# Earlier inputs, later weights and TensorE additions in the prologue of a Fourier-filter and mixer kernel

## The chip, the cores and the metric

One core of a Trainium2 chip. The metric is device time in microseconds (us), the median of several executions of the whole program. A ratio is the mean time of one kernel's runs over that of the other's of the same rounds on the same chip, so it is not quite the ratio of the medians quoted beside it.

Names: PE is TensorE, DVE is VectorE, ACT is ScalarE, POOL is GpSimd, SP is SyncE. PEld is a weight load of TensorE. "L216" is line 216 of the kernel in question; line numbers differ between kernels.

## The reference

```python
# x (8, 3008, 256); the four mixer weights arrive as float64
X = np.fft.rfft(x, axis=1)
y = np.fft.irfft(X * (filt_r + 1j * filt_i)[None], n=3008, axis=1)     # filter
h = np.maximum(y.transpose(0, 2, 1) @ w_tok1, 0.0) @ w_tok2             # w_tok1 (3008, 256)
u = y + h.transpose(0, 2, 1)
out = u + np.maximum(u @ w_ch1, 0.0) @ w_ch2
```

The kernel computes the transforms as matmuls in two factors (47 x 64): first transform, z through memory, filter, g through memory, then the mixer. The weights come as 64-bit numbers. The kernel reads them as pairs of 32-bit words and rounds each to float32 as the sum of two parts, "top" and "rest".

## The kernel before: the parts that matter

Instructions are issued to each engine in the order in which the program emits them. The prologue makes the first input's filter (`dft(GROUPS[0])`) and, between its steps, rounds the token weights tile by tile; each `next(convert)` rounds one tile and issues the load of a later one.

```python
    def rounded(st, n, parts, late=False):
        # ... both = a pair of buffers (hp holds two pairs), top and rest in it
        nc.scalar.activation(out=top, in_=hi_f, func=AF.Copy, scale=2.0 ** -112)      # ScalarE starts it
        nc.vector.tensor_scalar(out=top_i, ...)                                       # four VectorE steps
        nc.vector.scalar_tensor_tensor(out=top_i, ...)                                # top is ready here
        nc.vector.tensor_scalar(out=rest_i, ...)
        nc.vector.scalar_tensor_tensor(out=rest, ...)
        for src, dst in parts:
            nc.vector.tensor_tensor(out=dst, in0=src(top), in1=src(rest), op=ALU.add) # the addition

    def w1_fold(i):                      # w_tok1 alone: times the inverse transform's first factor
        nc.tensor.matmul(ps, wai_t, w, start=True, stop=True)
        nc.scalar.copy(out=w, in_=ps)

        # filter, one step k: b_unit(k) and bi_unit(k - 1)
        nc.tensor.matmul(ps, wbs[...], t2s[...])                  # ps_b, ps_pg
        nc.vector.tensor_tensor(out=p1, in0=ps, in1=fr, op=ALU.mult)
        nc.vector.scalar_tensor_tensor(out=p2[re], ...)           # - im * fi
        nc.vector.tensor_tensor(out=p2[im], ...)                  # re * fi
        nc.vector.tensor_tensor(out=p1, in0=p1, in1=p2, op=ALU.add)
        # ...
        nc.tensor.matmul(ps[0:KR], wis[...], prods.pop(k), start=True, stop=True)     # ps_acc
        nc.scalar.copy(out=t3s[c][:, r]..., in_=ps[0:KR]...)

        # prologue
        load(AHEAD)                                               # six weight tiles at once, then x
        # ... every step that converts:
                next(convert)                                     # round a tile, load another
                folds.append(len(folds))
                if len(folds) > 2:
                    w1_fold(len(folds) - 3)                       # then fold the tile of two steps ago
        # ... after the filter: w_tok2's 16 tiles
        for i in range(TC * N2 // NG):
            next(convert)
            if i == 2:
                acc = token_sums(0)                               # 48 products, 96 matmul instructions
        h1s[0] = token_relu(acc)
```

Of the kernel before, what the change touches and what calls it, by code (L numbers as in the profile page):

```python
# [45 lines left out]
AHEAD = 6  # L46
# [3 lines left out]
def _make_tables():  # L50








    n2 = np.arange(N2)
    wa = np.zeros((P, P))  # L60
    wai = np.zeros((P, P))
    for h in range(2):
        r = slice(h * 64, h * 64 + 64)
        for k2 in range(K2):
            th = 2 * np.pi * ((n2 * k2) % N2) / N2
            c, s = np.cos(th), np.sin(th)
            re, im = 4 * k2 + 2 * h, 4 * k2 + 2 * h + 1
            wa[r, re] = c
            wai[re, r] = c * (1.0 if k2 == 0 else 2.0)
            if k2 == 0:  # L70
                alt = 1.0 - 2.0 * (n2 % 2)
                wa[r, im] = alt
                wai[im, r] = alt
            else:
                wa[r, im] = -s
                wai[im, r] = -2.0 * s
    n1 = np.arange(N1)
    re = (n1 // A) * (2 * A) + n1 % A
    im = re + A
    wb = np.zeros((KR, K2, P))  # L80
    wi = np.zeros((P, K2, KR))
    for k2 in range(K2):
        for s in range(2 * A):
            if s < A:
                k, sign, q = k2 + 64 * s, 1.0, s
            else:
                j = s - A + 1
                k, sign, q = 64 * j - (k2 if k2 else 32), -1.0, 32 + s - A
                if j == A and k2:
                    continue  # L90
            th = 2 * np.pi * ((n1 * k) % N) / N
            c, sn = np.cos(th), np.sin(th)
            edge = k in (0, NF - 1)
            if edge:
                sn = np.zeros(N1)
            if k2:
                wb[re, k2, q] = c
                wb[im, k2, q] = sign * sn
                wb[re, k2, HALF + q] = -sn
                wb[im, k2, HALF + q] = sign * c  # L100
            else:
                src = re if s < A else im
                wb[src, k2, q] = c
                wb[src, k2, HALF + q] = -sn
                m = 1.0 if edge else 2.0
                wi[q, k2, src] = m * c
                wi[HALF + q, k2, src] = -m * sn
    wi[:, 1:, :] = wb[:, 1:, :].transpose(2, 1, 0)
    wi /= N
    f = np.float32  # L110
    return wa.astype(f), wai.astype(f), wb.astype(f), wi.astype(f)
# [3 lines left out]
def kernel(  # L115
# [13 lines left out]
    wa_np, wai_np, wb_np, wi_np = _make_tables()  # L129
# [4 lines left out]
    wi_d = nc.inline_tensor(wi_np, name="wi_t").ap()  # L134

# [32 lines left out]
    wai_t = glob.tile([P, P], FP32, name="wai_t")  # L168

# [35 lines left out]
    def rounded(st, n, parts, late=False):  # L205
# [3 lines left out]
        if late:  # L209

            top = p1p.tile([P, 512], FP32, tag="p1", name="top")[:, 0:n]
            rest = p2p.tile([P, 512], FP32, tag="p2", name="rest")[:, 0:n]
        else:
            both = hp.tile([P, 2, 512], FP32, tag="hh", name="both")
            top, rest = both[:, 0, 0:n], both[:, 1, 0:n]
# [9 lines left out]
        nc.vector.scalar_tensor_tensor(out=rest, in0=lo, scalar=2.0 ** -52, in1=rest, op0=ALU.mult, op1=ALU.mult)  # L225
        for src, dst in parts:
            nc.vector.tensor_tensor(out=dst, in0=src(top), in1=src(rest), op=ALU.add)

    def w1_load(i):
        st = stage(512)  # L230
        rows = moe_w_tok1.rearrange("(n2 n1) t -> n2 n1 t", n1=N1)
        last = 2 * i + 2 == A
        if last:
            nc.gpsimd.memset(st.bitcast(U32)[HALF:P, 512:1024], 0)
        for h in range(2):
            n = 1 if last and h else 2
            lo = h * A + 2 * i
            nc.gpsimd.dma_start(st[h * HALF:(h + 1) * HALF, 0:n * DT].rearrange("p (a t) -> p a t", t=DT),
                                rows[:, lo:lo + n, :])
        yield  # L240
        rounded(st, 512, [(lambda v: v, w1[:, 2 * i:2 * i + 2, :].rearrange("p a t -> p (a t)"))])

    def w1_fold(i):

        ps = bank("po%d" % (i % 2))
        w = w1[:, 2 * i:2 * i + 2, :].rearrange("p a t -> p (a t)")
        nc.tensor.matmul(ps, wai_t, w, start=True, stop=True)
        nc.scalar.copy(out=w, in_=ps)

    def w2_load(i):  # L250
# [16 lines left out]
        rounded(st, n, [(both, dst[:, :, :, ds(g * NG, NG)]), (some(w, 1), w2[:, t, ds(w * P + g * NG, NG)].unsqueeze(1))])  # L267
# [39 lines left out]
    def weights():  # L307

        steps = ([w1_load(i) for i in range(A // 2)] + [w2_load(i) for i in range(TC * N2 // NG)]
                 + [wc1_load(c * (DC // 512), False) for c in range(DH)])  # L310
        n = len(steps)
        steps += [f(i) for f, i in LAST]
        loads = iter(steps)

        def load(k):
            for _, s in zip(range(k), loads):
                next(s)

        load(AHEAD)
        yield  # L320
        for i, s in enumerate(steps):
            next(s, None)

            load(not n - 2 <= i < n)
            yield
# [5 lines left out]
    def x_load(b, c):  # L331
        last = c == NXC - 1
        t = xp.tile([P, XC, D], FP32, tag="x", name="x")
# [20 lines left out]
    def dft(bs):  # L354
# [3 lines left out]
        for u in todo[0:XB]:  # L358
            x_load(*u)
        for i, u in enumerate(todo):  # L360
            a_unit(*u, ("acc", "b")[i % 2] if first else "b")
            if i + XB < len(todo):
                x_load(*todo[i + XB])
# [16 lines left out]
        def b_unit(k):  # L380
# [7 lines left out]
            p1 = p1p.tile([P, nb, D], FP32, tag="p1", name="p1")  # L388
            p2 = p2p.tile([P, nb, D], FP32, tag="p2", name="p2")
# [3 lines left out]
            nc.vector.tensor_tensor(out=p1, in0=p1, in1=p2, op=ALU.add)  # L393
            prods[k] = p1

        def bi_unit(k):
            ps = bank("acc").rearrange("p (b d) -> p b d", b=2)[:, 0:nb, :]
            nc.tensor.matmul(ps[0:KR], wis[k // WC][:, k % WC, :], prods.pop(k), start=True, stop=True)  # L398
# [199 lines left out]
    def mix(b, next_ready, convert):  # L598
# [13 lines left out]
        for i in range(n + 1):  # L612
            now, old = i < n, i >= 1
            next(convert, None)
# [14 lines left out]
            next(convert, None)  # L629
# [29 lines left out]
    with tc.manual_schedule():  # L659
# [3 lines left out]
        convert = weights()  # L663
        next(convert)
        folds = []
        for i, _ in enumerate(dft(GROUPS[0])):
            if i == 0:
                for t, src in ((wai_t, wait_d), (wai, wai_d)):
                    nc.scalar.dma_start(t, src)

            if i % 2 == 1 and i < NXC or i % 3 == 2 and NXC < i <= NXC + 3 * (A // 4):
                next(convert)
                folds.append(len(folds))
                if len(folds) > 2:
                    w1_fold(len(folds) - 3)
        for c in range(A // TC4):
            t4_load(0, c)
        for i in range(TC * N2 // NG):
            next(convert)
            if i < 2:  # L680
                w1_fold(A // 2 - 2 + i)
            if i == 2:
                acc = token_sums(0)
        h1s[0] = token_relu(acc)
        for _ in range(DH):
            next(convert)
# [4 lines left out]
        for bs, after in zip(GROUPS, GROUPS[1:] + ((),)):  # L691
            todo = dft(after) if after else iter(())
            done = not after
            for b in bs:
# [3 lines left out]
                for i, _ in enumerate(mix(b, next_ready, convert)):  # L698
# [34 lines left out]
```

## Time and profile before

| | before |
|---|---|
| median, 4 runs | 2668.18 us (2663.97 to 2670.58) |
| stage A: to the first filter matmul | 62.0 us |
| stage B: to VectorE's last filter product | 83.2 us |
| tail: to VectorE's first sum for the mixer | 57.8 us (mixer starts at 203.1) |
| the mixer, to the end | 2464.8 us |

These borders are read from the timeline of the profiled run (span 2667.9 us). In all tables below they are taken in the same way: the first matmul on ps_b from t and wb, the start of the last filter product that writes p (the addition after it, where there is one, is not counted), the start of the first sum v from u. The prediction calls the tail stage C and counts to the mixer's first matmul (202.2 us), one us earlier. A timeline row reads: start, length, engine, line, operation, output<-input, shapes, count, and in brackets the idle time of that engine before the row with what ended it.

### The profile page before, as it was taken

Reading aid. Unit: us, or ns where it says so; the run is one execution under the profiler, and the core shown is the slowest. Engines: PE = TensorE matmul, PEld = TensorE weight load, DVE = VectorE, ACT = ScalarE, POOL = GpSimd, SP = SyncE. Lnnn points to the kernel's source line nnn. Section 1 sums busy time; section 2 is a strip of 40 time slices with the busy share of each in tenths; the row PEclk is TensorE's granted clock in tenths of the full one; section 3 lists DMA queues with packets and bytes.
Section 4 is the critical chain, followed back from the end, with each engine's and each line's share of the span. In section 5 each row is a group of like instructions: output and inputs, shape, how many; then the busy total and the mean of one; then the engine's idle time right before and its main releaser. Section 6 shows DMA issues by size and latency. Waiting matters only on the chain.

```text
span 2667.9 us, 31511 instructions
## 1 busy us (share of the span) xinstructions
PE 2511.5 (94%) x10840; PEld 1997.6 (75%) x10840; DVE 1825.9 (68%) x3505; ACT 677.4 (25%) x1325; POOL 503.4 (19%) x926
## 2 busy tenths in 40 slices
PE   4666999999999999999999999999999999999997
PEld 1344766687787777788877777788888888888886
DVE  3886588846567688745658588755678586647675
ACT  2222322212322222212322122222222122212221
POOL 2324211111212111121121112121121111211221
PEclk8778999999999999999999999999999999999999
DMA  8663344322332222212233223211322211100000
GB/s 219 190 188 111 114 119 122 96 77 79 96 103 83 72 78 75 70 32 63 90 99 89 66 84 85 79 33 41 103 70 79 55 46 56 24 9 8 17 15 17
DMA packets 167158, 210.28 MB, mean 79 GB/s; under 512 B 35868, under 2 KB 115633, under 8 KB 166998
## 3 DMA queue, kind: packets, MB, share of 16 engines
q1 hardware_dynamic: 92937, 111.56, 14.4%
q0 software_dynamic: 30976, 44.53, 6.9%
q10 hardware_dynamic: 43085, 52.17, 6.0%
q8 instruction: 86, 1.41, 0.2%
q14 instruction: 74, 0.61, 0.1%
HBM read 133.15 MB, written 74.97 MB: 78 GB/s over the span
## 4 chain that ended last, share of the span: by engine, by line
PE 71%; DVE 16%; issue 2%; ACT 2%; DMA 0%; SPq 0%; DVEq 0%; POOL 0%; ACTq 0%; POOLq 0%
PE ps_po L526 24%; PE ps_pg L492 14%; PE ps_pg L508 11%; PE ps_acc L452 6%; PE ps_acc L435 5%; DVE t L470 3%; PE ps_acc L457 3%; DVE hh L470 3%; PE ps_b L382 2%; PE ps_b L349 2%; PE ps_acc L398 2%; DVE u L470 2%; DVE s L470 2%; DVE p L392 1%; DVE p L391 1%
## 5 line engine op out<-in xcount | busy, mean ns | idle before, releaser
L470 DVE TENSOR_TENSOR hh<-ps_pg,s 128x512 f32<-128x512 f32 (+3 forms) x864 | 482.6, 586 | 639.7 <-ACT s L495 639.7
L571 POOL DMA_DIRECT2D out_dram<-r x757 | 409.7, 550 | 1971.5 <-ACT hh L513 855.6
L513 ACT ACTIVATE hh<-hh 128x512 f32<-128x512 f32 (+1 forms) x576 | 347.9, 621 | 1141.6 <-DVE hh L470 1141.6
L526 PE MATMUL ps_po<-t,wc 128*128 128x256 f32 (+1 forms) x2304 | 535.8, 375 | 3.7 <-DVE t L470 2.4
L526 PEld LDWEIGHTS ps_po<-t,wc 128*128 128x128 f32 x2304 | 434.4, 190 | 128.3 <-issue 50.4
L492 PE MATMUL ps_pg<-v,wc 128*128 128x256 f32 (+1 forms) x1728 | 417.5, 378 | 1.5 <-DVE v L470 1.5
L526 PE MATMUL ps_po<-hh,wc 128*128 128x256 f32 (+1 forms) x1728 | 413.3, 375 | 3.1 <-ACT hh L513 3.1
L492 PEld LDWEIGHTS ps_pg<-v,wc 128*128 128x128 f32 x1728 | 330.5, 192 | 42.5 <-DVE v L470 1.9
L526 PEld LDWEIGHTS ps_po<-hh,wc 128*128 128x128 f32 x1728 | 328.2, 190 | 42.2 <-ACT hh L513 5.1
L508 PE MATMUL ps_pg<-u,wc 128*128 128x256 f32 (+1 forms) x1152 | 294.3, 378 | 16.0 <-DVE hh L470 15.7
L470 DVE TENSOR_TENSOR t<-t,hh 128x256 f32<-128x256 f32 (+1 forms) x576 | 243.5, 423 | 19.8
L508 PEld LDWEIGHTS ps_pg<-u,wc 128*128 128x128 f32 x1152 | 215.3, 190 | 52.8 <-DVE hh L470 28.6
L470 DVE TENSOR_TENSOR s<-ps_pg,hh 128x512 f32<-128x512 f32 (+1 forms) x288 | 196.1, 681 | 30.0
L452 PE MATMUL ps_acc<-w,h 128*128 128x512 f32 (+1 forms) x384 | 181.7, 596 | 15.8 <-ACT h L441 11.6
L470 DVE TENSOR_TENSOR t<-hh 128x512 f32<-128x512 f32 (+1 forms) x288 | 193.1, 671 | 0.6 <-ACT hh L513 0.6
L435 PE MATMUL ps_acc<-t,w 128*128 128x256 f32 x768 | 169.5, 383 | 6.3 <-DMA t<-g_tmp 5.0
L492 PE MATMUL ps_pg<-u,wc 128*128 128x256 f32 (+1 forms) x576 | 172.4, 381 | 0.4 <-DVE hh L470 0.4
L398 PE MATMUL ps_acc<-p,wi 128*96 128x512 f32 (+1 forms) x320 | 148.2, 546 | 23.7 <-DVE p L393 12.3
L508 PE MATMUL ps_pg<-v,wc 128*128 128x256 f32 (+1 forms) x576 | 169.2, 375 | 0.0
L435 PEld LDWEIGHTS ps_acc<-t,w 128*128 128x128 f32 x768 | 147.1, 192 | 28.1 <-issue 5.8
L382 PE MATMUL ps_b<-t,wb 96*128 96x512 f32 (+1 forms) x288 | 132.7, 542 | 23.2 <-DVE p L392 11.4
L495 ACT COPY s<-ps_pg 128x256 f32<-128x256 f32 (+1 forms) x288 | 105.8, 367 | 148.6 <-PE ps_pg L492 144.5
(67 smaller groups left out, 1947.5 us busy)
## 6 DMA issues: line engine op xcount, KB each, us to landing
z_tmp<-t ACTq DMA_DIRECT2D x96, 256.0 KB
t<-z_tmp SPq DMA_DIRECT2D x128, 192.0 KB
g_tmp<-t ACTq DMA_DIRECT2D x128, 192.0 KB
t<-g_tmp SPq DMA_DIRECT2D x48, 512.0 KB
x<-in_x_dram SPq DMA_DIRECT2D x184, 128.0 KB
out_dram<-r POOLq DMA_DIRECT2D x698, 32.0 KB, 1.8
wb<-wb_t SPq DMA_DIRECT2D x80, 96.0 KB
wi<-wi_t SPq DMA_DIRECT2D x80, 96.0 KB
```

The lines of the kernel that those rows point to most:

```text
L382: nc.tensor.matmul(ps, wbs[k // WC][:, k % WC, :], t2s[k // KC][:, k % KC], start=True, stop=True)
L398: nc.tensor.matmul(ps[0:KR], wis[k // WC][:, k % WC, :], prods.pop(k), start=True, stop=True)
L435: nc.tensor.matmul(acc[:, t, :], w1[:, a, ts(t, P)], t4[b, a // TC4][:, a % TC4, :], start=(a == 0 and t == 0), stop=(a == A - 1 and t == ...
L452: nc.tensor.matmul(ps[:, 0:w], h1[:, t, ts(dh, P)], w2[:, t, ds(m * 512, w)], start=(t == 0), stop=False)
L457: nc.tensor.matmul(ps[:, ds(q * P, n)], t4[b, c][:, r, ts(dh, P)], wai[:, 0:n], start=False, stop=(q == 3))
L470: nc.vector.tensor_tensor(out=out, in0=in0, in1=in1, op=op)
L492: nc.tensor.matmul(ps[:, 0:hw], wc1[:, jp, n, :], mov, start=True, stop=True)
L495: nc.scalar.copy(out=s[:, 0], in_=g[0][:, 0, 0:hw])
L508: nc.tensor.matmul(ps[:, 0:hw], wc1[:, jp, n, :], mov, start=True, stop=True)
L513: nc.scalar.activation(out=hs, in_=hs, func=AF.Relu)
L526: nc.tensor.matmul(po[i][:, j, 0:hw], wc2[:, jp, n, :], mov, start=(jp == 0 and first == 1), stop=(jp == JP - 1 and last == 1))
L571: q.dma_start(rows[g, e, :, ds(h * A + 4 * m, n)], blocks[ts(g, CW), h, e, 0:n])
```

## The change

Its intent: let x arrive before the weights do, so that the filter starts earlier; and take work from VectorE, which is the fullest engine of the prologue, by letting TensorE add. A matmul accumulates in PSUM, so the product with top and the product with rest give the product with their sum. w_tok1 needed a product anyway; w_tok2 gets one with the identity. Likewise the filter's two products p1 and p2 are each multiplied by the second transform's factor and added in PSUM.

```diff
+    spare = [(hp, "hh"), (hp, "hh"), (rp, "r")]          # three buffer pairs
+    behind, banks = [], ["po%d" % i for i in range(4)]
+    def on_chip(stat, top, rest, n, parts):
+        # ... appended to behind, run later:
+            nc.tensor.matmul(ps, stat, top, start=True, stop=False)
+            nc.tensor.matmul(ps, stat, rest, start=False, stop=True)
+            for src, dst in parts:
+                nc.scalar.copy(out=dst, in_=src(ps))
     def w1_load(i):
+        q = nc.sync if i < EARLY else nc.gpsimd           # EARLY = 4
         ...
-        rounded(st, 512, [... w1 ...])
+        on_chip(wai_t, *halves(st, 512, spare_pair()), 512, [... w1 ...])
     def w2_load(i):
         ...
-        rounded(st, n, [... w2 ...])
+        on_chip(ident, *halves(st, n, spare_pair()), n, [... w2 ...])
+    def convert():
+        if len(behind) > 1:
+            behind.pop(0)()                               # matmuls and copy of two steps ago
+        round_tile()
+        load_tile()
     def x_load(b, c):
-        t = xp.tile(...)
+        where, tag = ((xp, "x"), (tp, "t"), (vp, "v"))[c % 3] if b == 0 else (xp, "x")
     def dft(bs):
-        for u in todo[0:XB]:                              # XB = 2
+        ahead = 3 * XB if first else XB
+        for u in todo[0:ahead]:
         def b_unit(k):
-            nc.vector.tensor_tensor(out=p1, in0=p1, in1=p2, op=ALU.add)
+            if not first:
+                nc.vector.tensor_tensor(out=p1, in0=p1, in1=p2, op=ALU.add)
         def bi_unit(k):
-            nc.tensor.matmul(ps[0:KR], wis[...], prods.pop(k), start=True, stop=True)
+            for i, p in enumerate(parts):
+                nc.tensor.matmul(ps[0:KR], wis[...], p, start=(i == 0), stop=(i == len(parts) - 1))
     # prologue: 3 roundings in stage A (before: 6), 11 in stage B (before: 6), 14 of w_tok2 in the tail (before: 16)
+            if i < NXC:
+                if i % 2 == 0 and 2 <= i: load_tile()
+                if i in (7, 9, 11): convert()
+            elif (i - NXC) % 3 == 2: convert()
+        for i in range(rounds, A // 2 + TC * N2 // NG):
+            convert()
+            if i == rounds + 2:
+                acc = token_sums(0)
```

(Cuts are marked with "..." and by comments. Left out: the identity table, the split of `rounded` into `halves` and the addition, and the removal of `w1_fold`, whose product `on_chip` now makes.)

More of the change, by code (lines that the diff above doesn't have):

```diff
@@ L45 @@
 NG = 8
-AHEAD = 6
+EARLY = 4
 GROUPS = ((0,), (1, 2), (3, 4), (5, 6), (7,))
@@ L110, in _make_tables @@
     f = np.float32
-    return wa.astype(f), wai.astype(f), wb.astype(f), wi.astype(f)
+    return wa.astype(f), wai.astype(f), wb.astype(f), wi.astype(f), np.eye(P, dtype=f)
 @with_exitstack
@@ L127 @@
     nc = tc.nc
-    wa_np, wai_np, wb_np, wi_np = _make_tables()
+    wa_np, wai_np, wb_np, wi_np, id_np = _make_tables()
     wa_d = nc.inline_tensor(wa_np, name="wa_t").ap()
@@ L134 @@
     wi_d = nc.inline_tensor(wi_np, name="wi_t").ap()
+    id_d = nc.inline_tensor(id_np, name="id_t").ap()
     z_d = nc.dram_tensor("z_tmp", (B, K2, KR, D), FP32, kind="Internal").ap()
@@ L168 @@
     wai_t = glob.tile([P, P], FP32, name="wai_t")
+    ident = glob.tile([P, P], FP32, name="ident")
     filts = [glob.tile([P, 2, KC, D], FP32, name="filt%d" % i) for i in range(FB)]
@@ L203, in stage, with halves @@
         return where.tile([P, n], I64, tag=tag, name="st")
-    def rounded(st, n, parts, late=False):
+    def halves(st, n, pair):
         words = [st.bitcast(t).rearrange("p (n w) -> p n w", w=2)[:, 0:n] for t in (U32, FP32)]
         lo, hi, hi_f = words[0][:, :, 0], words[0][:, :, 1], words[1][:, :, 1]
-        if late:
-            top = p1p.tile([P, 512], FP32, tag="p1", name="top")[:, 0:n]
-            rest = p2p.tile([P, 512], FP32, tag="p2", name="rest")[:, 0:n]
-        else:
-            both = hp.tile([P, 2, 512], FP32, tag="hh", name="both")
-            top, rest = both[:, 0, 0:n], both[:, 1, 0:n]
+        top, rest = (v[:, 0:n] for v in pair)
         top_i, rest_i = top.bitcast(U32), rest.bitcast(U32)
@@ L225, in rounded, with spare_pair, f @@
         nc.vector.scalar_tensor_tensor(out=rest, in0=lo, scalar=2.0 ** -52, in1=rest, op0=ALU.mult, op1=ALU.mult)
+        return top, rest
+    spare = [(hp, "hh"), (hp, "hh"), (rp, "r")]
+    def spare_pair():
+        where, tag = spare[0]
+        spare.append(spare.pop(0))
+        both = where.tile([P, 2, 512], FP32, tag=tag, name="both")
+        return both[:, 0], both[:, 1]
+    def rounded(st, n, parts, late):
+        if late:
+            pair = (p1p.tile([P, 512], FP32, tag="p1", name="top"), p2p.tile([P, 512], FP32, tag="p2", name="rest"))
+        else:
+            pair = spare_pair()
+        top, rest = halves(st, n, pair)
         for src, dst in parts:
             nc.vector.tensor_tensor(out=dst, in0=src(top), in1=src(rest), op=ALU.add)
+    behind, banks = [], ["po%d" % i for i in range(4)]
+    def on_chip(stat, top, rest, n, parts):
+        banks.append(banks.pop(0))
+        def f(tag=banks[0]):
+            ps = bank(tag)[:, 0:n]
+            nc.tensor.matmul(ps, stat, top, start=True, stop=False)
+            nc.tensor.matmul(ps, stat, rest, start=False, stop=True)
+            for src, dst in parts:
+                nc.scalar.copy(out=dst, in_=src(ps))
+        behind.append(f)
     def w1_load(i):
@@ L237, in w1_load @@
             lo = h * A + 2 * i
-            nc.gpsimd.dma_start(st[h * HALF:(h + 1) * HALF, 0:n * DT].rearrange("p (a t) -> p a t", t=DT),
-                                rows[:, lo:lo + n, :])
+            q.dma_start(st[h * HALF:(h + 1) * HALF, 0:n * DT].rearrange("p (a t) -> p a t", t=DT),
+                        rows[:, lo:lo + n, :])
         yield
-        rounded(st, 512, [(lambda v: v, w1[:, 2 * i:2 * i + 2, :].rearrange("p a t -> p (a t)"))])
-    def w1_fold(i):
-        ps = bank("po%d" % (i % 2))
-        w = w1[:, 2 * i:2 * i + 2, :].rearrange("p a t -> p (a t)")
-        nc.tensor.matmul(ps, wai_t, w, start=True, stop=True)
-        nc.scalar.copy(out=w, in_=ps)
+        on_chip(wai_t, *halves(st, 512, spare_pair()), 512,
+                [(lambda v: v, w1[:, 2 * i:2 * i + 2, :].rearrange("p a t -> p (a t)"))])
     def w2_load(i):
@@ L265, in both @@
             return bass.AP(tensor=v.tensor, offset=v.offset, ap=[v.ap[0], [A, 2], [1, w], [N1, NG]])
-        rounded(st, n, [(both, dst[:, :, :, ds(g * NG, NG)]), (some(w, 1), w2[:, t, ds(w * P + g * NG, NG)].unsqueeze(1))])
+        on_chip(ident, *halves(st, n, spare_pair()), n,
+                [(both, dst[:, :, :, ds(g * NG, NG)]), (some(w, 1), w2[:, t, ds(w * P + g * NG, NG)].unsqueeze(1))])
     def combine(w):
@@ L309, in weights, with load, rnd @@
         steps = ([w1_load(i) for i in range(A // 2)] + [w2_load(i) for i in range(TC * N2 // NG)]
-                 + [wc1_load(c * (DC // 512), False) for c in range(DH)])
-        n = len(steps)
-        steps += [f(i) for f, i in LAST]
-        loads = iter(steps)
-        def load(k):
-            for _, s in zip(range(k), loads):
-                next(s)
-        load(AHEAD)
-        yield
-        for i, s in enumerate(steps):
-            next(s, None)
-            load(not n - 2 <= i < n)
-            yield
+                 + [wc1_load(c * (DC // 512), False) for c in range(DH)] + [f(i) for f, i in LAST])
+        loads, rounds = iter(steps), iter(steps)
+        def load():
+            s = next(loads, None)
+            if s:
+                next(s)
+        def rnd():
+            s = next(rounds, None)
+            if s:
+                next(s, None)
+        return load, rnd
+    load_tile, round_tile = weights()
+    def convert():
[3 more added lines that the diff above has]
+        load_tile()
     xs = {}
@@ L332, in x_load @@
         last = c == NXC - 1
-        t = xp.tile([P, XC, D], FP32, tag="x", name="x")
+        where, tag = ((xp, "x"), (tp, "t"), (vp, "v"))[c % 3] if b == 0 else (xp, "x")
+        t = where.tile([P, XC, D], FP32, tag=tag, name="x")
         rows = x[b].rearrange("(n2 n1) d -> n2 n1 d", n1=N1)
@@ L361, in dft @@
             a_unit(*u, ("acc", "b")[i % 2] if first else "b")
-            if i + XB < len(todo):
-                x_load(*todo[i + XB])
+            if i + ahead < len(todo):
+                x_load(*todo[i + ahead])
             yield
@@ L387, in b_unit @@
             fi = t[im, 1, k % KC, :].unsqueeze(1).to_broadcast([HALF, nb, D])
-            p1 = p1p.tile([P, nb, D], FP32, tag="p1", name="p1")
-            p2 = p2p.tile([P, nb, D], FP32, tag="p2", name="p2")
+            p1 = p1p.tile([P, 2 if first else nb, D], FP32, tag="p1", name="p1")
+            if first:
+                p1, p2 = p1[:, 0:1], p1[:, 1:2]
+                prods[k] = (p1, p2)
+            else:
+                p2 = p2p.tile([P, nb, D], FP32, tag="p2", name="p2")
+                prods[k] = (p1,)
             nc.vector.tensor_tensor(out=p1, in0=ps, in1=fr, op=ALU.mult)
@@ L392, in b_unit @@
             nc.vector.tensor_tensor(out=p2[im], in0=ps[re], in1=fi, op=ALU.mult)
-            nc.vector.tensor_tensor(out=p1, in0=p1, in1=p2, op=ALU.add)
-            prods[k] = p1
+            if not first:
+                nc.vector.tensor_tensor(out=p1, in0=p1, in1=p2, op=ALU.add)
         def bi_unit(k):
             ps = bank("acc").rearrange("p (b d) -> p b d", b=2)[:, 0:nb, :]
-            nc.tensor.matmul(ps[0:KR], wis[k // WC][:, k % WC, :], prods.pop(k), start=True, stop=True)
+            parts = prods.pop(k)
+            for i, p in enumerate(parts):
+                nc.tensor.matmul(ps[0:KR], wis[k // WC][:, k % WC, :], p, start=(i == 0), stop=(i == len(parts) - 1))
             c, r = divmod(k, KC)
@@ L596, in one_step, with mix @@
             todo_v.pop(0)()
-    def mix(b, next_ready, convert):
+    def mix(b, next_ready):
         wait = [0]
@@ L613, in mix @@
             now, old = i < n, i >= 1
-            next(convert, None)
+            convert()
             if now:
@@ L628, in mix @@
                 down(mo, jo, 0, hhs[i - 1], tts[i - 1], pos.setdefault(mo, []))
-            next(convert, None)
+            convert()
             if now:
@@ L662 @@
             nc.vector.memset(t, 0.0)
-        convert = weights()
-        next(convert)
-        folds = []
+        rounds = 0
         for i, _ in enumerate(dft(GROUPS[0])):
             if i == 0:
-                for t, src in ((wai_t, wait_d), (wai, wai_d)):
+                for t, src in ((wai_t, wait_d), (ident, id_d), (wai, wai_d)):
                     nc.scalar.dma_start(t, src)
-            if i % 2 == 1 and i < NXC or i % 3 == 2 and NXC < i <= NXC + 3 * (A // 4):
-                next(convert)
-                folds.append(len(folds))
-                if len(folds) > 2:
-                    w1_fold(len(folds) - 3)
+            if i < NXC:
+                if i % 2 == 0 and 2 <= i:
+                    load_tile()
+                if i in (7, 9, 11):
+                    convert()
+                    rounds += 1
+            elif (i - NXC) % 3 == 2:
+                convert()
+                rounds += 1
         for c in range(A // TC4):
             t4_load(0, c)
-        for i in range(TC * N2 // NG):
-            next(convert)
-            if i < 2:
-                w1_fold(A // 2 - 2 + i)
-            if i == 2:
+        for i in range(rounds, A // 2 + TC * N2 // NG):
+            convert()
+            if i == rounds + 2:
                 acc = token_sums(0)
+        for f in behind:
+            f()
+        behind.clear()
         h1s[0] = token_relu(acc)
         for _ in range(DH):
-            next(convert)
+            convert()
         for dh in range(DH):
@@ L696, in next_ready @@
                     return b != bs[-1] or done
-                for i, _ in enumerate(mix(b, next_ready, convert)):
+                for i, _ in enumerate(mix(b, next_ready)):
                     if not done and i % len(bs) == 0:
```

## The prediction

> **What bounds the kernel now.** I read the page first. Its slices show TensorE at nine tenths or more from the fifth slice to the last but one, so the mixer, some 2465 of 2668 us, is TensorE's. The first four slices are different:
>
> ```profile
> PE   4666999999999999999999999999999999999997
> DVE  3886588846567688745658588755678586647675
> DMA  8663344322332222212233223211322211100000
> ```
>
> A slice is 66.7 us. The change touches what lies before the mixer, plus nothing of weight in it, so I looked for where the mixer starts: in the timeline its first matmul (ps_pg from u and wc) begins at 202.2 us. That span of 202 us has three stages, whose borders I took from the timeline (first filter matmul 62.0, last filter product 146.2). The windows view, with busy time per engine, granted clock, DMA share and GB/s:
>
> ```profile
> 0.00:62.00 62.00, 25.95 (x32) 7.69 (x32) 20.31 (x33) 14.15 (x23) 19.35 (x40) 0.92 0.84 223
> 62.00:147.00 85.00, 57.15 (x141) 32.65 (x142) 70.19 (x158) 18.41 (x44) 24.75 (x44) 0.74 0.64 177
> 147.00:203.00 56.00, 36.33 (x126) 26.30 (x124) 47.79 (x106) 12.87 (x25) 18.94 (x33) 0.76 0.63 195
> ```
>
> Stage A (0 to 62, first transform): no engine is full (VectorE 20 of 62), the DMAs are. In the DMA view of this stage the slices from 4 to 40 us stand at 230 to 243 GB/s with a share of nine tenths and over. The groups of TensorE say the same, 24.8 + 4.3 us of waits for x.
>
> Stage B (62 to 147, filter): VectorE has 70 of 85 us. Its groups, and TensorE's:
>
> ```profile
> L393 DVE TENSOR_TENSOR p<-p,p 128x256 f32<-128x256 f32 x32 | 13.6, 425 | 1.1
> L390 DVE TENSOR_TENSOR p<-ps_b,filt 128x256 f32<-128x256 f32 x16 | 6.7, 421 | 8.5 <-PE ps_b L382 4.9 <-DMA filt<-in_filt_r_dram 3.0 <-DMA g_tmp<-t 0.4
> L227 DVE TENSOR_TENSOR w<-both 128x512 f32<-128x512 f32 x6 | 4.2, 692 | 0.2
> L398 PE MATMUL ps_acc<-p,wi 128*96 128x256 f32 x64 | 28.1, 532 | 23.7 <-DVE p L393 12.3 <-issue 8.9 <-ACT t L403 2.1
> ```
>
> L393 and L227 are the two additions that the change hands to TensorE. L398 shows TensorE waiting for VectorE.
>
> Stage C (147 to 203): 16 roundings of w_tok2 and two of w_ch1 on VectorE, back to back, one every 2.73 us; TensorE does the token sums beside them. The timeline has the sums, and the activation that closes them, in:
>
> ```profile
> 153.65 23.02 PE L435 MATMUL ps_acc<-t,w 128*128 128x256 f32 x96 [4.98 <-DMA t<-g_tmp]
> ...
> 187.65 0.58 ACT L441 ACTIVATE h<-ps_acc 128x512 f32<-128x512 f32 x1
> ```
>
> The first line: sums from 153.65 to 176.7, released by a transfer. The second: their activation comes 11 us late, because ScalarE takes it in program order after the roundings' steps. That hurts nobody today; the order itself will matter below.
>
> **What the Trainium skill says.** "TensorE: Matmul & The Clock Gate", step-by-step section of Part 2, says that only weight loads are pulled ahead and matmuls stay in program order; its Part 1 (architectural detail) says ScalarE and VectorE are strict FIFO. The trace agrees: the activation at 187.65 above. The same page, Part 1 on the clock gate, says the clock halves when TensorE idles. The trace agrees in kind: the granted mean is 0.74 in stage B, and a 128x512 product (two instructions) took 1.02 us at 54.2 but 1.91 us at 83.05. "DMA: Bandwidth & Descriptors", "Issuing engines are not separate DMA queues", says that all queues share the same 16 engines; so moving four w_tok1 loads to another queue gives no bandwidth, only another order. Stage A agrees: three queues together, never much over 240 GB/s.
>
> **Part 1: six x tiles in flight, weights later (stage A).** Before, the stage carries x 3.1 MB, z 3.1 MB and all twelve w_tok1 tiles of 0.52 MB, 12.5 MB; at 238 GB/s that is 52 us, and the stage takes 62 with start and turnaround. After, by the code, three tiles (4, 5, 6) still go out at time zero on GpSimd's queue, which has nothing ahead of them, four sit between the x loads, one more follows the first rounding. Some 6.5 tiles compete before the last z is written: 9.6 MB, 40 us. The first filter matmul then comes at about 49 instead of 62: **-13 us**. The number in flight itself gains little, since bandwidth, not latency, is the limit.
>
> **Part 2: the filter stage.** VectorE loses 32 additions of 0.44 us with gap (14.2 us): a unit is 3 operations, 1.32 us, not 1.76. A rounding loses its addition: 2.36 us for 512 columns, 1.9 for 376. But the stage holds 11 roundings (9 of w_tok1, 2 of w_tok2), not 6. VectorE's work: 32 x 1.32 + 9 x 2.36 + 2 x 1.9 = 67 us, against 70. So its work hardly falls.
>
> The waits rise. Each convert() now emits first the two matmuls of the tile rounded two steps ago, ScalarE's copy of their result, and only then the next tile's rounding, which starts on ScalarE. ScalarE is FIFO, so the rounding waits for the copy, that for the two matmuls, and those stand in TensorE's order behind the second filter product of the unit before, which waits for VectorE. From the end of p(k-1): the product of its second part, two instructions, 0.64 us at the fast clock and 1.14 at the slow (rows of L398; the first part's product can run earlier, as its operand is VectorE's first of three results); two 128x512 products, 1.88 us at the fast clock (at 146.79 in the timeline, x4), 3.6 at the slow; copy 0.58 + ACTIVATE 0.66 + handovers 0.1. Sum at a middle clock: 0.9 + 2.6 + 1.35 = about 4.8. VectorE has p(k), 1.32 us, to do meanwhile: some 3.5 us idle in each of ten converts, 35 us (2.6 each at full clock, 4.8 at half). In the kernel before, the same chain had only one product and the copy after the rounding, and cost 0.68 us at 84.85.
>
> 67 + 35 + 5 left of today's 9.8 us of waits for TensorE and filter transfers = 107 us, against 84: **+23 us**.
>
> **Part 3: the tail.** 14 w_tok2 roundings are left instead of 16, each 1.9 us on VectorE instead of 2.73: if VectorE stayed full, 14 us would be won. But the roundings now need TensorE, and the token sums are emitted after the third of them. The third to fourth convert's matmuls then stand behind 96 sum matmuls that wait for g. I count from the end of the filter products, T0 (146.2 before). Sums start at T0+7.5 and end at T0+30.5, as in the trace. VectorE does three roundings by about T0+8 and idles till the first matmuls after the sums, the copy and the ACTIVATE: T0+33.4. Eleven roundings follow. Two roundings are in flight, so a pair takes 1.9 + (matmuls 1.4 to 2.65 + two copies 0.75 + ACTIVATE 0.6): 4.7 to 5.9 us, 2.35 to 2.95 each, 28 us: T0+61. Last matmuls, copies and relu 3 us, the two u units some 11 us as before (192.6 to 203.1): mixer at T0+75, where it was T0+56: about **+18 us**.
>
> **Sum.** -13 + 23 + 18 = +28 us. I take 8 off, as a choice: part of the new waits will fall where VectorE waits for z or filter data anyway, a fuller TensorE should get the fast clock more often, and the hand-picked steps (7, 9, 11) suggest someone tuned this with a result in view. 2670.5 + 20 = **2690 us**. The mixer I leave unchanged: its roundings keep the addition on VectorE.
>
> **Rivals.**
> (1) VectorE stays the bound and is relieved. For it: 70 of 85 and 48 of 56 us busy. Then B falls to 75, C to about 42: with A some -35 us, 2635. Against it: the FIFO chain above.
> (2) TensorE becomes the bound of B at the slow clock. Its needed streaming is about 32 x 1.28 + 18 = 59 us at full clock, 118 at half. For it: clock 0.74 now. It would give +35 to +45 in B and about 2715.
> (3) DMA hides everything: the loads taken from A come back in B (4 w_tok1 tiles and one more w_tok2, 2.5 MB, 10 us at 238 GB/s). Stage B has a share of 0.64, so room; if it bites, A's gain is only moved, and the total is 2680 to 2700.
> (4) The whole is masked: impossible for the prologue, as the mixer needs h and u; whatever moves 202.2 moves the end.
>
> **Range and chances.** My uncertainties: A -5 to -18, B -8 to +40, tail -10 to +22. They don't add fully: 2655 to 2722 should hold 8 in 10. Two per cent is 53 us: faster than 2617 would need more than rival 1 gives; slower than 2724 needs rival 2 with the tail's full loss. So faster 0.02, same 0.94, slower 0.04.
>
> **What the profile after would show.** Right: first filter matmul near 49; gaps of about 3.5 us on VectorE ahead of each rounding's first operation in B, released by the ACTIVATE; an idle of some 20 us on VectorE while the sums run; mixer's start near 222. Wrong: VectorE dense in B or during the sums, or a first filter matmul still near 60. What would make it wrong most easily is the clock: full clock takes some 10 us from B, half adds 15.

## The result, and the profile after

| | before | after | difference |
|---|---|---|---|
| median, 4 runs each | 2668.18 us | 2693.3 us (2692.52 to 2694.26) | +25.1 |
| ratio | | 1.0096 (95%: 1.0079 to 1.0114) | |
| stage A | 62.0 | 52.5 | -9.5 |
| stage B | 83.2 | 109.5 | +26.3 |
| tail | 57.8 | 64.2 | +6.4 |
| mixer to the end | 2464.8 | 2466.3 | +1.5 |

The kernel is slower by about one per cent. The windows view of the kernel after, over its own three stages, with busy time per engine (PE, PEld, DVE, ACT, POOL; in brackets the number of instructions), granted TensorE clock, DMA share and GB/s:

```profile
0.00:52.50 52.50, 23.32 (x29) 6.74 (x29) 9.45 (x15) 10.77 (x17) 10.99 (x24) 0.82 0.88 236
52.50:162.40 109.90, 84.05 (x234) 49.65 (x234) 63.36 (x140) 23.81 (x53) 29.47 (x54) 0.82 0.58 155
162.40:226.20 63.80, 55.83 (x188) 33.52 (x188) 30.81 (x67) 17.97 (x53) 14.30 (x27) 0.97 0.52 165
```

VectorE (the third figure after the length) has less work than before, 63 and 31 us where it had 70 and 48, and longer stages. It waits. What for is in the timeline of stage B, here one convert (transfers and weight loads left out):

```profile
93.82 1.82 PE L440 MATMUL ps_acc<-p,wi 128*96 128x256 f32 x4
...
94.96 0.42 DVE L431 TENSOR_TENSOR p<-ps_b,filt 64x256 f32<-64x256 f32 x1
95.47 1.02 PE L250 MATMUL ps_po<-both,wai_t 128*128 128x512 f32 x2
...
96.33 1.02 PE L251 MATMUL ps_po<-both,wai_t 128*128 128x512 f32 x2
...
97.39 0.58 ACT L253 COPY w<-ps_po 128x512 f32<-128x512 f32 x1 [1.35 <-PE ps_po L251]
...
97.87 0.67 ACT L215 ACTIVATE both<-st 128x512 f32<-128x512 f32 x1
...
98.58 0.43 DVE L216 TENSOR_SCALAR both<-both 128x512 uint32<-128x512 uint32 x1 [3.20 <-ACT both L215]
```

VectorE ends a product at 95.38. The next thing in its program is the rounding of a tile, which ScalarE must begin (L215). ScalarE may not, as its program has the copy L253 first; the copy needs the two matmuls L250 and L251, of an older tile; these follow the filter product L440. The rounding at 98.58 needs nothing of all this: another tile, another buffer. VectorE idles 3.20 us, and so in every convert (2.88 to 3.74 us over the stage). In the kernel before, whose code starts the rounding ahead of the fold, the same step waited little:

```profile
84.85 0.43 DVE L220 TENSOR_SCALAR both<-both 128x512 uint32<-128x512 uint32 x1 [0.68 <-ACT both L219]
```

In the tail, the rows of VectorE and of TensorE around the token sums:

```profile
169.37 0.35 DVE L216 TENSOR_SCALAR both<-both 128x376 uint32<-128x376 uint32 x1 [0.19 <-ACT both L215]
...
195.27 0.36 DVE L216 TENSOR_SCALAR both<-both 128x376 uint32<-128x376 uint32 x1 [23.99 <-ACT both L215]
```

```profile
170.33 22.65 PE L477 MATMUL ps_acc<-t,w 128*128 128x256 f32 x96 [2.02 <-DMA t<-g_tmp]
192.81 0.80 PE L250 MATMUL ps_po<-both,ident 128*128 128x376 f32 x2
...
196.36 0.87 PE L250 MATMUL ps_po<-both,ident 128*128 128x376 f32 x2 [0.86 <-DVE both L217]
```

The sums run from 170.33 to 192.98, and VectorE stands still for 24 us, until the first rounding matmuls after them have been copied out. Before, the same 23 us of sums lay beside VectorE's roundings and cost nothing. The last row answers a question of size: the first of the two matmuls is released by L217, VectorE's second step, that is, as soon as top is there and before rest is.

### The profile page after: what moved, and what is told of

Same layout as the page of the kernel before. It is cut to its first block, busy times and chain, and to the rows that moved or that the text cites. A ratio compares the mean times of both kernels' runs of the same rounds, so it can differ in the third digit from the quotient of the medians.

```text
span 2692.5 us, 31796 instructions
## 1 busy us (share of the span) xinstructions
PE 2554.7 (95%) x10992; PEld 2024.4 (75%) x10992; DVE 1792.7 (67%) x3429; ACT 684.4 (25%) x1357; POOL 499.4 (19%) x918
## 4 chain that ended last, share of the span: by engine, by line
PE 71%; DVE 16%; issue 2%; ACT 2%; DVEq 0%; DMA 0%; ACTq 0%; POOL 0%; SPq 0%; POOLq 0%
PE ps_po L568 24%; PE ps_pg L534 14%; PE ps_pg L550 11%; PE ps_acc L494 6%; PE ps_acc L477 5%; DVE t L512 3%; PE ps_acc L499 3%; DVE hh L512 3%; PE ps_b L382 3%; PE ps_b L416 2%; PE ps_acc L440 2%; DVE u L512 2%; DVE s L512 2%; DVE p L431 1%; DVE p L430 1%
## 5 line engine op out<-in xcount | busy, mean ns | idle before, releaser
L512 DVE TENSOR_TENSOR t<-hh 128x512 f32<-128x512 f32 (+1 forms) x288 | 192.7, 669 | 0.6 <-ACT hh L555 0.6
L440 PE MATMUL ps_acc<-p,wi 128*96 128x256 f32 (+1 forms) x384 | 167.0, 530 | 25.9 <-DVE p L429 13.4
L537 ACT COPY s<-ps_pg 128x256 f32<-128x256 f32 (+1 forms) x288 | 105.8, 367 | 151.2 <-PE ps_pg L534 146.6
```

The costliest lines, as they stand in the source:

```text
L440: nc.tensor.matmul(ps[0:KR], wis[k // WC][:, k % WC, :], p, start=(i == 0), stop=(i == len(parts) - 1))
L512: nc.vector.tensor_tensor(out=out, in0=in0, in1=in1, op=op)
L537: nc.scalar.copy(out=s[:, 0], in_=g[0][:, 0, 0:hw])
```

## The experiments

Twelve kernels, each correct, each beside the kernel before on the same chip in the same rounds (that kernel's median in the three batches: 2666.72, 2667.08, 2667.48 us). The theory: **the order in which the engines' programs were written holds the roundings up, once behind two matmuls and a copy in stage B, once behind the token sums in the tail.** The rivals: the added matmuls are too much work for TensorE; VectorE's work still decides; the loads or the number of x tiles in flight decide.

### e1_order: round first, then the older tile's matmuls

```diff
     def convert():
-        if len(behind) > 1:
-            behind.pop(0)()
         round_tile()
+        if len(behind) > 2:
+            behind.pop(0)()
         load_tile()
```

> The changed kernel with one order swapped: a convert step rounds its tile first and only then emits the matmuls and copy of the tile rounded two steps ago. Same work on every engine. Theory (ScalarE's program order makes each rounding wait for two matmuls and a copy): VectorE's idle ahead of a rounding in the filter stage falls from about 3.2 us to about 0.5, the stage from 110 us to some 85, the total to about 2667 (2660 to 2675), near the kernel before. Rival (the added matmuls are too much work for TensorE at the clock it gets): the cycle of three units stays at 9.5 to 10.2 us and the total at 2685 or over.

Measured: 2672.89 us, ratio to before 1.0024 (1.0012 to 1.0037), against 1.0096 for the changed kernel. Same instructions, another order: three quarters of the loss are gone, stage B is 96.1 us instead of 109.5, with the granted clock up from 0.82 to 0.88. The rival of too much TensorE work falls. The stage did not reach the 85 us I expected, and the total stands inside the range written down only by its upper edge. In the group of each rounding's first step over stage B, the idle before it (last column) went from 28.7 to 21.5 us for the nine w_tok1 tiles (first row: the changed kernel, second row: e1_order):

```profile
L216 DVE TENSOR_SCALAR both<-both 128x512 uint32<-128x512 uint32 x9 | 3.8, 427 | 28.7 <-ACT both L215 28.7
L216 DVE TENSOR_SCALAR both<-both 128x512 uint32<-128x512 uint32 x9 | 3.8, 427 | 21.5 <-ACT both L215 21.5
```

Most converts now wait 0.8 to 1.4 us, but four wait 2.6 to 6.5 us. The timeline of e1_order around the longest:

```profile
70.07 0.37 ACT L445 COPY t<-ps_acc 96x256 f32<-96x256 f32 x1 [1.92 <-DMA g_tmp<-t]
...
74.92 0.32 ACTq L450 DMA_DIRECT2D g_tmp<-t  x1
...
75.34 0.66 ACT L215 ACTIVATE both<-st 128x512 f32<-128x512 f32 x1 [4.91 <-DMA t<-z_tmp]
```

ScalarE (ACTq is its queue) finishes a copy at 70.44 and stands until it issues a store of g at 74.92; the rounding's L215 comes after that. What the store itself waits for, these rows do not show. This led to e7.

### e2_w2_vector: w_tok2 added on VectorE, as before

```diff
-        on_chip(ident, *halves(st, n, spare_pair()), n, [... w2 ...])
+        rounded(st, n, [... w2 ...], False)
+        while behind:
+            behind.pop(0)()
```

> The changed kernel, but w_tok2's tiles are added on VectorE as before (no matmul, no copy for them). Theory (in the tail the roundings stand behind the token sums in TensorE's order, so VectorE idles 24 us): the idle goes, VectorE works through 14 roundings of 2.73 us beside the sums, the mixer starts 13 us earlier: about 2680 (2676 to 2685). Rival (the tail is bound by VectorE's work, which the matmuls relieve): 14 additions of 0.83 us come back, 12 us slower, about 2705.

Measured: 2675.91 us, ratio 1.0038 (1.0024 to 1.0052), a little better than written. The tail fell from 64.2 to 52.0 us; VectorE has no idle of over 5 us in it, though it does 14 more additions of two parts each. The relief of VectorE in the tail cost more than it gave.

### e3_sums_pieces: the token sums in twelve pieces

```diff
-            if i == rounds + 2:
-                acc = token_sums(0)
+            if i == rounds + 2:
+                pieces = sums_in_pieces(0, 2)      # the same 96 matmuls, two of 24 blocks at a time
+            if i >= rounds + 2:
+                acc = next(pieces)
```

> The changed kernel with the token sums of the first input not in one block but in twelve pieces of two blocks, one after each of the last twelve roundings' converts. Same work on every engine. Theory (a block of 96 matmuls in TensorE's fixed order holds up the roundings behind it): the 24 us idle of VectorE is spread and mostly gone, TensorE is then nearly full in the tail (about 21 us of rounding matmuls and 21 of sums), mixer 8 to 11 us earlier: about 2684 (2680 to 2687). Rival (TensorE's total work in the tail decides, the order does not): within 3 us of the changed kernel.

Measured: 2683.99 us, ratio 1.0063 (1.0051 to 1.0076). The tail fell to 55.4 us, by 8.8. The same work in finer turns: so it is the order of the sums and the roundings, not their amount, that cost this.

### e4_loads_alone: only the earlier x and later weights

All three additions are back on VectorE and each rounding comes ahead of the older fold; x in flight, load queues and schedule are those of the change. Essentially:

```diff
-        on_chip(wai_t, *halves(st, 512, spare_pair()), 512, [... w1 ...])
+        rounded(st, 512, [... w], False)           # and one fold matmul, copy, appended to behind
```

(with e1's order, e2's w_tok2 and e5's filter sum.)

> Only the first half of the change: six x tiles in flight ahead of the weights and the later schedule of loads and roundings; all three additions are back on VectorE and each rounding comes before the older tile's matmul, as in the kernel before. Theory (stage A carries fewer bytes and gains 9 us, but the five roundings moved out of A and the tail into the filter stage, which VectorE bounds, cost 13 there and give 5 back in the tail): 2667 (2660 to 2675), no gain. Rival (early x is a real gain that the TensorE additions then spoil): 2655 or under.

Measured: 2667.37 us, ratio 1.0002 (0.9989 to 1.0014): no gain. Stage A 52.3 us, B 96.7, tail 52.2: the ten microseconds won at the start come back in the filter stage as the roundings that were moved into it (11 against 6; VectorE is busy 83 of 97 us there), less what the tail then lacks.

### e5_products_vector: the filter's products added on VectorE, as before

```diff
-            if not first:
-                nc.vector.tensor_tensor(out=p1, in0=p1, in1=p2, op=ALU.add)
+            nc.vector.tensor_tensor(out=p1, in0=p1, in1=p2, op=ALU.add)     # and one product in bi_unit
```

> The changed kernel, but the two products of the first filter are added on VectorE as before (32 additions of 0.43 us back, 32 second matmul pairs gone). Theory (the additions taken from VectorE in the filter stage are paid back as waits: VectorE idles about 0.75 us for the next product in each cycle, and the convert's wait shrinks by what VectorE works longer): the stage changes by less than 5 us, total within 5 us of the changed kernel. Rival (VectorE's work bounds the stage and the matmul pairs relieve it): 14 us slower, about 2706.

Measured: 2693.39 us, ratio 1.0097 (1.0082 to 1.0113), the same as the changed kernel. Its groups of VectorE in stage B:

```profile
L429 DVE TENSOR_TENSOR p<-p,p 128x256 f32<-128x256 f32 x31 | 13.2, 425 | 1.1
...
L216 DVE TENSOR_SCALAR both<-both 128x512 uint32<-128x512 uint32 x9 | 3.8, 427 | 22.9 <-ACT both L215 22.9
```

13.2 us of additions are back in the window, the idle before roundings fell from 28.7 to 22.9 and the wait for a product from about 0.75 to about 0.45 us in each cycle (three filter steps and a convert): stage B is 110.9 us instead of 109.5. So taking these 32 additions from VectorE was worth nothing here. One rival to the reason stands untested: in both kernels the cycle takes some 10.2 us, and the granted clock falls to half once in each, for 3.4 us in every 10.24 (in the changed kernel from 92.2 to 95.6 and from 102.4 to 105.8 us). Whether this rhythm holds the cycle at its length, whatever VectorE has to do, no run shows.

### e6_order_mixed_tail: e1 plus additions where they are free

```diff
+        if beside_sums:
+            rounded(st, n, parts, False)
+        else:
             on_chip(ident, *halves(st, n, spare_pair()), n, parts)
     ...
             if i == rounds + 2:
+                while behind:
+                    behind.pop(0)()
                 acc = token_sums(0)
+                beside_sums.append(True)
+            if i == rounds + 10:
+                beside_sums.clear()
```

> e1_order plus a mixed tail: roundings that fall beside the token sums (eight of them) add on VectorE, those before and after on TensorE, and what waits is emitted ahead of the sums. Theory: VectorE's 21 us idle beside the sums goes, the tail falls from 58.9 us to about 48, total about 2662 (2657 to 2667), faster than the kernel before. Rival (the tail's length is set by work, not by the order): 8 additions of 0.8 us come back, 2675 or over.

Measured: 2659.32 us, ratio 0.9971 (0.9959 to 0.9984). The tail is 47.6 us, as expected, ten shorter than before the change.

### e7_order_filter_queue: e1 with the first filter's loads off ScalarE's queue

```diff
-            filt_load(c, (nc.sync, nc.scalar, nc.gpsimd) if first else (nc.sync,) * 3)
+            filt_load(c, (nc.sync, nc.gpsimd, nc.gpsimd) if first else (nc.sync,) * 3)
```

> e1_order with the first filter's loads taken off ScalarE's queue (they go out on GpSimd's). In e1_order 21.5 us of VectorE's idle ahead of roundings stay, where I expected 5. Theory: ScalarE is held up by its own issues of filter transfers, so the idle falls to about 10 us and the total to some 2663 (2658 to 2668). Rival (ScalarE waits for TensorE or for its g writes whatever else it issues): within 3 us of e1_order, 2670 to 2676.

Measured: 2654.38 us, ratio 0.9955 (0.9943 to 0.9968), better than the range written down. Stage B is 80.0 us instead of e1's 96.1; the idle before the nine roundings is down to 7.3 us, TensorE's clock is 0.97 and the transfers run at 216 GB/s instead of 177 (group and window of the stage):

```profile
L216 DVE TENSOR_SCALAR both<-both 128x512 uint32<-128x512 uint32 x9 | 4.2, 465 | 7.3 <-ACT both L215 7.3
...
49.70:130.00 80.30, 69.49 (x234) 39.22 (x234) 63.68 (x140) 23.86 (x52) 51.33 (x93) 0.97 0.82 216
```

The stores of g no longer hold ScalarE up: one goes out at 66.39, right after its copy ends at 66.36. Of the 18.5 us won against e1 (20.0 between the two profiled runs), 15.7 are won by the mixer's start. Another 5 lie at the very end and are a separate thing, see e12.

### e8_all_three: e6 and e7 together

> e6 and e7 together: the order swapped, the mixed tail, the filter loads off ScalarE's queue. If the parts add up: about 2653 (2647 to 2660), some 13 us under the kernel before. If the filter queue does nothing: as e6, about 2662.

Measured: 2641.41 us, ratio to the kernel before 0.9903 (0.989 to 0.9917): better than the range written down, as e7 alone had been. Taken from what was measured, the parts just add up (e1's 2672.89 less e6's 13.6 and e7's 18.5 is 2640.8). This version beats both kernels. Its three stages in the windows view:

```profile
0.00:50.70 50.70, 23.69 (x28) 6.76 (x29) 9.45 (x15) 11.53 (x18) 16.34 (x34) 0.81 0.88 238
50.70:132.40 81.70, 71.66 (x234) 40.18 (x234) 63.85 (x140) 23.89 (x52) 51.34 (x93) 0.95 0.82 212
132.40:179.00 46.60, 40.81 (x156) 28.40 (x156) 37.26 (x82) 14.53 (x37) 14.31 (x27) 0.96 0.71 226
```

VectorE's work in the filter stage is that of the changed kernel (63.85 against 63.36 us); it now takes 81.7 us, not 109.9. The mixer starts at 179.0 us, where it started at 203.1 and 226.2.

### e9_before_filter_queue: the kernel before with e7's line alone

> Control: the kernel before with only the filter loads taken off ScalarE's queue. Theory: there the filter stage is VectorE's (70 of 85 us busy), so at most its some 10 us of waits can go: 2662 to 2667. Rival (that queue is worth its 18 us in any kernel): about 2649.

Measured: 2660.57 us, ratio 0.9975 (0.9963 to 0.9988): 6.9 us, a little under the range. The mixer starts 7.6 us earlier, the stretch from there to the second input's token sums takes 2.7 us more (358.0 instead of 355.3), and the last segment of the run is 5.2 us shorter (as in e12). So e8 gains 19 us over this kernel too; the queue is not the whole of it.

### e10_two_in_flight: the changed kernel with two x tiles in flight

```diff
-        ahead = 3 * XB if first else XB
+        ahead = XB
```

> The changed kernel with two x tiles in flight as before, all else as changed. Theory (stage A is bound by the bytes that pass, not by how many x loads are open): the first filter matmul moves by under 3 us from 52.5, total within 3 us of the changed kernel. Rival (latency: six in flight is what won the 9.5 us): first filter matmul back near 60, total about 2701.

Measured: 2694.03 us, ratio 1.0102 (1.0088 to 1.0116), as the changed kernel. The row that begins stage B, here and in the changed kernel (52.47 us):

```profile
52.35 1.19 PE L416 MATMUL ps_b<-t,wb 96*128 96x256 f32 x2 [3.53 <-issue]
```

Six tiles in flight are worth nothing in the end. They do bring the last x matmul earlier (it ends at 42.1 us, here at 46.3), but the stretch from there to the first filter matmul is longer by the same (10.3 us, here 6.0). Stage A's 9.5 us come from what both kernels have: fewer and later weight tiles and roundings.

### e11_all_products_vector: e8 with e5's undoing

> e8_all_three, with the filter products added on VectorE again. In the changed kernel that addition was worth nothing (e5: 2693.4 against 2693.3). Theory (its worth was hidden by ScalarE's waits, which e8 has removed, so VectorE now bounds the stage): 9 to 14 us slower than e8, about 2652. Rival (it never bounds): as e8, 2638 to 2644.

Measured: 2648.77 us, ratio 0.9934 (0.9922 to 0.9947), 7.4 us over e8; stage B 86.1 us against 81.3. The same 32 additions that were worth nothing in the changed kernel are worth 7 us (5 of them by the mixer's start) once the wait ahead of the roundings is away. I had expected 9 or more, so they are not wholly on the path even then.

### e12_filter_queue_only: the changed kernel with e7's line alone

> The changed kernel with only the filter loads off ScalarE's queue, the order of a convert as changed. Theory (here a rounding waits for matmuls and copy, whatever ScalarE issues): 3 us or less gained, 2689 to 2694. Rival (ScalarE's transfer issues were the cause of the waits all along, the order only shifts them): 15 us or more gained, under 2678.

Measured: 2684.48 us, ratio 1.0066 (1.0052 to 1.008): 8.8 us under the changed kernel, where I expected 3 or less. The prologue agrees with the theory: stage B is 109.2 us against 109.5, and its roundings wait as before, for instance

```profile
106.23 0.43 DVE L216 TENSOR_SCALAR both<-both 128x512 uint32<-128x512 uint32 x1 [3.21 <-ACT both L215]
```

The mixer starts 2.9 us earlier, 2.3 of it from stage A. The rest lies elsewhere: 1.8 us in the third segment between the inputs' token sums, and 5.0 us in the last segment (299.7 us instead of 304.7), at whose end the run stops some 2.5 us after its last transfers instead of some 8. All five traces with this line (e7, e8, e9, e11, e12) have it, with 299.7 to 300.1 us, and none of the nine without it does (304.6 to 305.3). What ends the run earlier I could not settle. So in any comparison with and without this line, 5 us are not the prologue's.

### The parts together

| kernel | median us | ratio to before | A | B | tail | mixer starts |
|---|---|---|---|---|---|---|
| before | 2668.18 | 1 | 62.0 | 83.2 | 57.8 | 203.1 |
| after | 2693.3 | 1.0096 | 52.5 | 109.5 | 64.2 | 226.2 |
| e1 order | 2672.89 | 1.0024 | 51.5 | 96.1 | 58.9 | 206.5 |
| e3 sums in pieces | 2683.99 | 1.0063 | 51.8 | 108.6 | 55.4 | 215.7 |
| e4 loads alone | 2667.37 | 1.0002 | 52.3 | 96.7 | 52.2 | 201.1 |
| e6 e1 + mixed tail | 2659.32 | 0.9971 | 50.6 | 94.4 | 47.6 | 192.7 |
| e7 e1 + filter queue | 2654.38 | 0.9955 | 49.7 | 80.0 | 61.1 | 190.8 |
| e8 all three | 2641.41 | 0.9903 | 50.7 | 81.3 | 47.1 | 179.0 |

## Why the prediction was right, point by point

The class ("same", a change of under two per cent), the number (2690 against 2693.3) and the main mechanism came out. Its terms did so less well, and two of their errors cancel. That the total came within 4 us is in part luck.

- **Stage A, -13 forecast, -9.5 measured.** That the number in flight is not the limit is shown by e10; that the bytes are is argued from the DMA share (0.88). The bytes were misjudged: the DMA view has 13.8 MB in the stage before and 12.3 after, where the prediction had 12.5 and 9.6. Its slices were also read as too even: those of 230 to 243 GB/s end at some 17 us, later ones run from 26 to 399, so "never much over 240" holds for means over many slices only (223 for the stage). And of the four weight tiles on SyncE's queue, which were to sit between the x loads, two go out after the last x, ahead of the filter's loads (34.4 to 41.5 us). The last x matmul ended 12.2 us earlier, but the turnaround from there to the first filter matmul is 10.3 us (42.1 to 52.5), where it was 7.7 (54.3 to 62.0). That the two tiles are the cause fits e10, where no weight tile stands there and the turnaround is 6.0 us, but is not proven: the first filter matmul comes no earlier in e10.
- **Stage B, +23 forecast, +26.3 measured.** The chain runs as written down: 3.2 us of idle in a typical convert against 3.5. e1 shows that the order makes it. What the working lacked is an idle of about 0.75 us in each cycle ahead of one product, after TensorE has stood for some 2.3 us and runs slower; waits for products come to some 8 us in the stage, where 5 were forecast. VectorE's work hardly fell, as said.
- **Tail, +18 forecast, +6.4 measured.** This is the term that was mis-sized. The stop behind the sums is there: VectorE resumes 33 us after the last filter product, as forecast. But the eleven roundings that follow take 21.7 us (195.27 to 216.95), 1.97 each, not 28. I let the two matmuls begin when a rounding ends; the first begins at its middle, when top is ready (the row at 196.36). And the two u units (the products at the end of the tail that make u) took 7.1 us (219.03 to 226.16), not 11, at a granted clock of 0.97 in the tail.
- **The 8 us taken off** were to stand for waits that fall together and a better clock. The clock was better (0.73 to 0.82 in B, 0.76 to 0.97 in the tail), but B came out longer than its sum, not shorter. The discount was right in amount because the tail was overstated.
- **The rivals.** VectorE as the bound in the changed kernel: refuted by e5 (13 us of work came back and the stage grew by 1.4). TensorE's work as the bound: refuted by e1. Transfers given back in B: the share there is 0.58 in the kernel after, lower than before, so no. That whoever tuned the steps had a gain in view was no evidence: the gain was there to be had (e8), but for the order.

## What to carry to other kernels

Before an operation is moved to another engine, write down every engine's program around it and ask which unrelated instruction will now stand behind it; the order of two independent statements was worth 20 us here, and the additions taken from VectorE in the filter stage nothing until it was right. In a software pipeline, emit what starts the next item ahead of what finishes the old one. Long blocks on an in-order engine (96 matmuls, 23 us) belong in pieces, or beside work that does not need this engine.

## What the Trainium skill lacked or had wrong

- "DMA: Bandwidth & Descriptors", "Issuing engines are not separate DMA queues", says that issuing on several engines only saves sequencer time. It lacks the other side: an engine's compute waits in line behind its own transfer issues. In e1_order ScalarE stood from 70.44 to 74.92 us ahead of one issue, with a rounding behind it; taking the first filter's loads off its queue shortened the filter stage from 96.1 to 80.0 us (e7).
- "TensorE: Matmul & The Clock Gate", "Why this matters for your kernels", asks for no TensorE gap of over some 3 us. In the kernel after, gaps of about 2.3 us were enough: after each, a pair of 256-column matmuls took 1.17 us where 0.64 was seen just before, and the fast rate was back some 3.4 us later (92.2 to 95.6 in one cycle).
- That a loop's cycle and the clock's changes can fall into one period, no page says: in the kernel after and in e5 the clock was half for 3.4 us in every 10.24 us, and the loop's cycle took some 10.2 us in both, though their VectorE work differs by 12 us over the stage. Which sets which is open.
- No page has the 5 us at the end of the run that went with one queue's loads (e12); its cause is open.
